# Hashed attention with two MLPs: first pair's bits written straight into the operand, query hashes on four column groups, every second weight tile of the second MLP converted during the second job

## The chip, the cores and the metric

One core of a Trainium2 chip runs the whole program; the other cores are idle. The metric is the device time of one execution in microseconds (us), and the profile is one execution taken by the hardware profiler. Engines: PE is TensorE, DVE is VectorE, ACT is ScalarE, POOL is GpSimd, SP is SyncE, which here only issues DMAs. ACT issues a few DMAs too. Each engine runs its own instructions strictly in the order in which the program was written.

## The reference

```python
q_bits = (einsum('bhsd,dk->bhsk', q, proj) > 0)          # 6 bits a row, k_bits likewise
mask = q_bucket[:, :, :, None] == k_bucket[:, :, None, :]
scores = where(mask, scale * q @ k.T, -1e9)
attn = softmax(scores); x = attn @ v                     # 2 batches, 8 heads, 768 rows, 64 wide
h = x @ w_in;  g = s * relu(h)**2 + b;   y = g @ w_out   # first MLP: 1536 tokens, 512 -> 2048 -> 512
h = y @ w2_in; g = h * clip(h + 3, 0, 6) / 6; out = g @ w2_out
```

Everything is float32. The weights arrive as raw 64-bit words.

## The kernel before, in words

**Split products.** PE takes each float32 operand in two parts, a rounded one ("hi") and a rest ("lo"). ACT makes the hi parts, POOL and DVE the lo parts.

**Attention.** The 1536 rows are four units of 384 query rows (two per batch), and each unit has four pairs of heads: 16 pairs, number g. A pair's operands are four tiles. `KA` holds k_hi in partitions 0 to 63 and from 64 on the hash bits of the keys; `QA` has q_hi and the hash bits of the queries; `KB` and `QB` hold the lo parts and a shifted copy. A matmul over `KA` and `QA` then adds a huge number wherever two hashes differ. So a pair's first score matmul (L466) waits for its key bits, its query bits, `k_shift` (a DMA that copies k_hi into the upper half of `KB`) and `k_lo`, `q_lo` on POOL. Each pair has six slots; a slot is scores with a row maximum on DVE (L472), then the transposed scores (L519), exponentials on ACT (L525, tile `P`), a cast (L532, `pt`), the rest on POOL (L538) and the product with v (L548). `v_scale` is seven DVE instructions that wait for the load of v (`vP`).

**Hash bits.** `bits_mm` (L382) multiplies a projection of 32 columns with 384 columns of k or q at a time; each such matmul uses its own group of 32 output columns of PE (four for k, two for q). `bits` (L391) compares with 0 on DVE into a tile `bits`; for the keys `bits_big` (L397) scales it on ACT. Then DMAs move the rows: `bits_in` (L415, four DMAs for each of the first four pairs), `bits_out` (L407, two DMAs for q; L403 stores key bits in DRAM for the second unit of the batch, which fetches them in L419). The four pairs of the first unit have operand sets of their own, set up by `ones_rows` (L329, L330).

**MLPs.** Tokens of a unit pass through an MLP as one job of 32 weight tiles of 128x512; the eight jobs run in the order of `ORDER`: MLP 1 on units 0 and 1 (jobs 0 and 1), MLP 2 on units 0 and 1 (jobs 2 and 3), and so on. A tile's 12 matmuls (L681) take some 2.1 us. In the first 16 tiles of a job each result goes through ACT, DVE, ACT, DVE (L692 to L716) into `G`. The first job of each MLP (job 0 and job 2) converts its weights from 64-bit words: load `wr` (L612, 512 KB), two ACT operations (`w_exp` L618, `w_low` L627), two DVE operations (L631, L636), and a store of the float32 tile (L642, 256 KB). Later jobs fetch that (L646). A tile sits in one of four buffers `wf` until `w_hi` on ACT (L651) and `w_lo` on POOL (L657) have split it.

**Order.** `Plan` is a list scheduler in the kernel's own Python. Each step has an engine, a due time, a duration and the things it needs, and the plan writes all instructions in the order that it finds; DMAs are put on SP's queue, some on ACT's. Any changed step or duration may reorder every engine.

Of the kernel before, what the change touches and what calls it, by code (L numbers as in the profile page):

```python
# [226 lines left out]
def attn_moe_moe2(ctx, tc, qT, kT, vT, proj, cvec, eye, w1_in, w1_out, w2_in, w2_out, out):  # L227
# [36 lines left out]
    cv = const.tile([128, 4], F32, name="cv")  # L264
# [5 lines left out]
    ones = const.tile([128, 32], F16, name="ones")  # L270
    hbit = {(b, h): dr_p.tile([128, 384], F32, name=f"kb{b}{h}") for b in range(2) for h in range(4)}
# [28 lines left out]
    def bank(g):  # L300
        if small_ring(g) == "mm":
            return ps["mm"].tile([128, 512], F32, tag="mm", name="small")
        return ps["S"].tile([128, 512], F32, tag="S", name="S")
# [54 lines left out]
    def k_lo(g):  # L358
        nc.gpsimd.tensor_tensor(out=operand(g, "KB")[0:64], in0=pd[g]["k"], in1=operand(g, "KA")[0:64].bitcast(F32), op=ALU.subtract)  # L359
# [17 lines left out]
    def bits_mm(g, nm):  # L377
        n = 4 if nm == "k" else 2
        src = pd[g][nm][0:64].rearrange("p h n -> p (h n)")
        bp = bank(g)  # L380
        for i in range(n):
            nc.tensor.matmul(out=bp[32 * i:32 * i + 32, 0:384], lhsT=projb, rhs=src[:, 384 * i:384 * i + 384],  # L382
                             start=True, stop=True)
        pd[g][nm + "ps"] = bp

    def bits(g, nm):


        n, i = (128, 0) if nm == "k" else (64, 1)
        bt = ev_p.tile([128, 384], F32R, tag="r" if nm == "k" else "o", name="bits")  # L390
        nc.vector.tensor_scalar(out=bt[0:n], in0=pd[g][nm + "ps"][0:n, 0:384], scalar1=0.0, scalar2=cv[0:n, i:i + 1],  # L391
# [7 lines left out]
    def bits_out(g, nm):  # L399
        bt = pd[g][nm + "bt"]  # L400
        if nm == "k":
            u, hp = pairs[g]
            queue[0].dma_start(out=hbit[units[u][0], hp], in_=bt.bitcast(F32))  # L403
        else:
            dst = operand(g, "QA").rearrange("p h n -> p (h n)").bitcast(F32)
            for i in range(2):
                queue[0].dma_start(out=dst[64:64 + 2 * NB, 384 * i:384 * i + 384],  # L407
                                  in_=bt[32 * i:32 * i + 2 * NB].bitcast(F32))

    def bits_in(g):  # L410
        u, hp = pairs[g]
        if g < 4:
            dst = operand(g, "KA").rearrange("p h n -> p (h n)").bitcast(F32)
            for i in range(4):
                queue[0].dma_start(out=dst[64:64 + 2 * NB, 384 * i:384 * i + 384], in_=pd[g]["kbt"][32 * i:32 * i + 2 * NB].bitcast(F32))  # L415
            return
# [354 lines left out]
    for e in range(4):  # L771
        add("DVE", 9.0 * e - 14.0, 2.0, ones_rows, (e,), gives=[("ones", e)])
# [3 lines left out]
    for g in range(NP):  # L776
# [7 lines left out]
        add("DMA", t, (0.6, 1.7), load_k, (g,), acq=[(kH, g)], gives=[("k", g)])  # L784
        add("DMA", t, (1.2, 1.7), load_q, (g,), acq=[(qD, g)], gives=[("q", g)])
        add("ACT", t, 1.47, k_hi, (g,), needs=free + [("k", g)], gives=[("kh", g)])
        add("DMA", t, (0.6, 1.7), k_shift, (g,), needs=[("kh", g)], gives=[("kd", g, 0)])
# [192 lines left out]
```

## Time and profile before

| | |
|---|---|
| median of 3 runs | 876.61 us (875.98 to 876.70) |
| profiled execution, its own time | 876.93 us |
| its span (first to last instruction) | 875.1 us |
| PE busy / ACT / POOL / DVE | 95% / 66% / 65% / 53% of the span |
| jobs 0, 1, 2, 3 begin their matmuls at | 101.8, 261, 354, 457 us |

Busy shares are means over the whole span. What a change is worth is read from the stage where it stands: from 0 to 101.8 us there is attention alone, then jobs with attention slots between their tiles, and in the last third nearly only weight tiles.

### The profile page before, as it was taken

How to read it: one execution, taken by the hardware profiler on the slowest of the kernel's cores; microseconds unless marked ns; L12 is line 12 of the kernel's file. 1: busy time of each engine (PE TensorE's matmuls, PEld its weight loads, DVE VectorE, ACT ScalarE, POOL GpSimd, SP SyncE). 2: the span in 40 equal slices, each digit the busy share in tenths (PEclk: the TensorE clock that was granted, in tenths of full speed). 3: DMA queues.
4: the chain of work that ended last, by engine and by line, in shares of the span. 5: the costliest groups of instructions: out<-in, count | busy, mean ns of one | idle time of the engine just before them, and what ended most of it. 6: DMA issues, size and time to landing. Idle time of an engine off the chain costs nothing.

```text
span 875.1 us, 15178 instructions
## 1 busy us (share of the span) xinstructions
PE 828.4 (95%) x5430; PEld 735.1 (84%) x5430; DVE 464.2 (53%) x838; ACT 579.0 (66%) x977; POOL 572.3 (65%) x388
## 2 busy tenths in 40 slices
PE   6779898999999799998999999999999999999998
PEld 2446677869786799887899987999998888999998
DVE  7668758788755741897365404530465422521520
ACT  5359959898785554898887635753687464743752
POOL 5467757678687256455877656566588675666664
PEclk9779999999999899999999999999999999999999
DMA  8874356677668435787855434444334323444442
GB/s 189 164 185 149 110 157 189 219 225 224 199 181 175 125 105 188 266 264 269 273 172 156 129 113 129 135 133 126 119 96 116 79 79 88 129 126 128 124 142 76
DMA packets 74987, 136.72 MB, mean 156 GB/s; under 512 B 20288, under 2 KB 30880, under 8 KB 74912
## 3 DMA queue, kind: packets, MB, share of 16 engines
q1 hardware_dynamic: 73516, 133.09, 52.2%
q10 hardware_dynamic: 1396, 2.66, 1.3%
q8 instruction: 43, 0.70, 0.4%
q14 instruction: 32, 0.26, 0.1%
HBM read 103.86 MB, written 21.54 MB: 143 GB/s over the span
## 4 chain that ended last, share of the span: by engine, by line
PE 80%; DVE 7%; DMA 5%; ACT 4%; issue 2%; POOL 1%; SPq 1%; ACTq 0%; DVEq 0%; POOLq 0%
PE mm L681 58%; PE T L519 6%; PE S L466 6%; PE pv L548 6%; DMA kH<-k_t 2%; PE S L559 1%; DMA wr<-w_in 1%; PE S L382 1%; DMA vP<-v_t 1%; PE pv L580 1%; DVE nh L472 1%; DVE wf L631 1%; ACT wf L627 1%; DVE am L425 1%; DVE KA L330 1%
## 5 line engine op out<-in xcount | busy, mean ns | idle before, releaser
L657 POOL TENSOR_TENSOR wl<-wf,wh 128x512 fp32r<-128x512 f32 x256 | 330.2, 1292 | 197.5 <-ACT wh L651 183.2
L681 PE MATMUL mm<-X,wh 128*128 128x384 f32 x1024 | 267.4, 342 | 13.4 <-DVE G L713 6.8
L681 PE MATMUL mm<-G,wh 128*128 128x384 f32 x1024 | 265.5, 340 | 0.0
L651 ACT CAST wh<-wf 128x512 fp32r<-128x512 f32 x256 | 157.7, 617 | 107.9 <-PE mm L681 77.3
L538 POOL TENSOR_TENSOR pt<-P,pt 128x768 f16<-128x768 f32 x96 | 159.8, 1668 | 79.4 <-ACT pt L532 71.1
L681 PEld LDWEIGHTS mm<-X,wh 128*128 128x128 f32 x1024 | 186.0, 191 | 23.9 <-DVE G L713 9.8
L681 PEld LDWEIGHTS mm<-G,wh 128*128 128x128 f32 x1024 | 182.6, 188 | 11.4 <-issue 10.4
L681 PE MATMUL mm<-X,wl 128*128 128x384 f32 x512 | 173.7, 339 | 0.0
L681 PE MATMUL mm<-G,wl 128*128 128x384 f32 x512 | 171.5, 335 | 0.0
L472 DVE TENSOR_REDUCE nh<-S 128x1 f32<-128x384 f32 x192 | 103.3, 552 | 90.9 <-PE S L466 89.8
L525 ACT ACTIVATE P<-T 128x768 f32<-128x768 f32 x96 | 78.0, 812 | 49.3 <-PE T L519 46.8
L681 PEld LDWEIGHTS mm<-X,wl 128*128 128x128 f32 x512 | 97.4, 190 | 0.0
L681 PEld LDWEIGHTS mm<-G,wl 128*128 128x128 f32 x512 | 96.1, 188 | 0.0
L466 PE MATMUL S<-KA,QA 76*128 76x384 f32 x192 | 72.8, 379 | 14.2 <-DVE nh L472 10.4
L532 ACT CAST pt<-P 128x768 f16<-128x768 f32 x96 | 80.0, 834 | 7.9 <-PE pv L548 5.9
L519 PE MATMUL T<-QA,KA 108*128 108x384 f32 x192 | 69.0, 359 | 3.4 <-ACT pt L532 1.2
L466 PE MATMUL S<-KB,QB 128*128 128x384 f32 x192 | 67.4, 351 | 0.3 <-DMA KB<-KA 0.3
L519 PE MATMUL T<-QB,KB 128*128 128x384 f32 x192 | 65.7, 342 | 0.0
L466 PEld LDWEIGHTS S<-KA,QA 76*128 76x128 f32 x192 | 37.4, 195 | 31.2 <-DVE nh L472 21.1
L548 PE MATMUL pv<-pt,vt 128*64 128x384 f16 x576 | 63.3, 344 | 0.2 <-DVE X L596 0.2
L631 DVE SCALAR_TENSOR_TENSOR wf<-wm,wf 128x512 int32<-128x512 int32 x64 | 43.9, 686 | 33.2 <-ACT wf L627 26.7
L359 POOL TENSOR_TENSOR KB<-kH,KA 64x1536 fp32r<-64x1536 f32 x14 | 48.6, 3473 | 11.4 <-ACT KA L353 11.2
(358 smaller groups left out, 942.0 us busy)
## 6 DMA issues: line engine op xcount, KB each, us to landing
wf<-w SPq DMA_DIRECT2D x192, 256.0 KB
wr<-w_in SPq DMA_DIRECT2D x32, 512.0 KB
w<-wf SPq DMA_DIRECT2D x64, 256.0 KB
wr<-w_out SPq DMA_DIRECT2D x31, 512.0 KB
KB<-KA SPq DMA_DIRECT2D x16, 384.0 KB
qD<-q_t SPq DMA_DIRECT2D x28, 192.0 KB
kH<-k_t SPq DMA_DIRECT2D x13, 384.0 KB
U<-ur SPq DMA_DIRECT2D x16, 192.0 KB
```

What stands on the lines that cost most here:

```text
L359: nc.gpsimd.tensor_tensor(out=operand(g, "KB")[0:64], in0=pd[g]["k"], in1=operand(g, "KA")[0:64].bitcast(F32), op=ALU.subtract)
L466: nc.tensor.matmul(out=sp[:, 0:NQ], lhsT=operand(g, Q)[0:n, h, 128 * t:128 * t + 128], rhs=operand(g, K)[0:n, h, NQ * j:NQ * j + NQ], star ...
L472: nc.vector.reduce_max(out=maxima[g % 2][:, j, c:c + 1], in_=sd.pop((s, j))[:, 0:NQ], axis=AX.X, negate=True)
L519: nc.tensor.matmul(out=tp[:, j, 0:NQ], lhsT=operand(g, K)[0:n, h, c:c + 128], rhs=operand(g, Q)[0:n, h], start=(a == 0), stop=(a == 1))
L525: nc.scalar.activation(out=P, in_=td.pop((g, k))[:, :, 0:NQ], func=AF.Exp, scale=0.125)
L532: (nc.scalar.copy if THI(g) == "ACT" else nc.vector.tensor_copy)(pd[g][h][:, 0, 2 * i:2 * i + 2], pd[g]["P", k])
L538: e.tensor_tensor(out=pt[:, 1, 2 * i:2 * i + 2], in0=pd[g].pop(("P", k)), in1=pt[:, 0, 2 * i:2 * i + 2], op=ALU.subtract)
L548: nc.tensor.matmul(out=d["pv"][64 * h:64 * h + 64, 0:NQ], lhsT=vt[:, vc, 64 * h:64 * h + 64], rhs=d[h][:, a, c], start=(c == 0 and n == 0) ...
L631: nc.vector.scalar_tensor_tensor(out=d["wf"], in0=d["mt"], scalar=-2147483648, in1=d["wf"], op0=ALU.bitwise_and, op1=ALU.bitwise_or)
L651: nc.scalar.copy(hi.rearrange("p a b -> p (a b)"), wq[key]["wf"])
L657: nc.gpsimd.tensor_tensor(out=lo.rearrange("p a b -> p (a b)"), in0=d["wf"], in1=d["hi"].rearrange("p a b -> p (a b)").bitcast(F32), op=AL ...
L681: nc.tensor.matmul(out=a, lhsT=w[:, k, :], rhs=src[k][:, xi, :], start=(k0 + k == 0 and p == 0), stop=(k0 + k == nk - 1 and p == 2))
```

## The change

For pair 0 the key and query bits go from PSUM to their operand rows in six DVE instructions of 12 partitions (no ACT scaling, no bit DMAs); the keys use a negated projection `projk`, and the stored copy for pair 4 is read from `KA`. Query hashes of pairs 4 to 15 use four column groups of 192 columns in place of two of 384, and four DMAs in place of two. `k_lo` is cut into one instruction per head. 12 warm-up matmuls stand in place of 16. Odd tiles of MLP 2 are converted during job 1, stored, and fetched in job 2. Several durations in the planner's table are smaller.

```diff
-WARM = (16, 6)
+WARM = (12, 6)
...
+EARLY = 2
...
-    def k_lo(g):
-        nc.gpsimd.tensor_tensor(out=operand(g, "KB")[0:64], in0=pd[g]["k"], in1=operand(g, "KA")[0:64].bitcast(F32), op=ALU.subtract)
+    def k_lo(g, h):
+        nc.gpsimd.tensor_tensor(out=operand(g, "KB")[0:64, h], in0=pd[g]["k"][:, h], in1=operand(g, "KA")[0:64, h].bitcast(F32), op=ALU.subtract)
...
     def bits_mm(g, nm):
-        n = 4 if nm == "k" else 2
+        n, w = (2, 384) if nm == "q" and g < 4 else (4, 384 if nm == "k" else 192)
...
     def bits(g, nm):
...
+        if g == 0:
+            ps_, dst = pd[g][nm + "ps"], operand(g, "KA" if nm == "k" else "QA").rearrange("p h n -> p (h n)")
+            for i in range(4 if nm == "k" else 2):
+                r = slice(32 * i, 32 * i + 2 * NB)
+                a, b = (cv[r, 4:5], cv[r, 5:6]) if nm == "k" else (0.0, cv[r, 1:2])
+                nc.vector.tensor_scalar(out=dst[64:64 + 2 * NB, 384 * i:384 * i + 384], in0=ps_[r, 0:384], scalar1=a, scalar2=b,
+                                        op0=ALU.is_ge if nm == "k" else ALU.is_gt, op1=ALU.mult if nm == "k" else ALU.subtract)
+            return
...
-            for i in range(2):
-                queue[0].dma_start(out=dst[64:64 + 2 * NB, 384 * i:384 * i + 384],
-                                  in_=bt[32 * i:32 * i + 2 * NB].bitcast(F32))
+            w = 384 if g < 4 else 192
+            for i in range(2 * NQ // w):
+                queue[0].dma_start(out=dst[64:64 + 2 * NB, w * i:w * i + w],
+                                  in_=bt[32 * i:32 * i + 2 * NB, 0:w].bitcast(F32))
...
+        if g == 4:
+            queue[0].dma_start(out=operand(g, "KA")[64:64 + 2 * NB].rearrange("p h n -> p (h n)").bitcast(F32), in_=hrow)
+            return
...
+            pre = (m, jn) == (1, first[1]) and i % EARLY == EARLY - 1
             if jn == first[m]:
...
+                if pre:
+                    ck, tw, use, order = (100, i), M[jn - 1][0] + i * M[jn - 1][1], past(jn - 1, i, 0), []
...
-                last = [("wf", ck, 2)]
...
+                last = [("wf", ck, 1 if pre else 2)]
...
-            else:
...
+            if jn != first[m] or pre:
```

How the order moves is shown at three places. First, SP's queue from the shift of pair 0 on, before. `KB_151<-KA_149` is the shift of pair 0, `KA_153` and `QA_154` are operands of pair 1, `KA_160` and later ones of pairs 2 and 3; `kb` are key bits going to DRAM.

```order
L356 DMA KB_151<-KA_149 64x1536
L415 DMA KA_149<-bits 12x384 x4
L407 DMA QA_150<-bits 12x384 x2
L335 DMA kH<-k_t 64x1536
L403 DMA kb_117<-bits 128x384
L343 DMA qD<-q_t 64x2x384 x2
L356 DMA KB_155<-KA_153 64x1536
L335 DMA kHx<-k_t 64x1536
L356 DMA KB_162<-KA_160 64x1536
L415 DMA KA_153<-bits 12x384 x4
L403 DMA kb_118<-bits 128x384
```

The same stretch of SP's queue after; pair 0 has `KA_151`, `KB_153`, pair 1 has `KA_155`, `QA_156`, `KB_157`.

```order
L362 DMA KB_153<-KA_151 64x1536
L349 DMA qD<-q_t 64x2x384 x2
L362 DMA KB_157<-KA_155 64x1536
L416 DMA kr<-KA_151 12x1536
L341 DMA kH<-k_t 64x1536
L341 DMA kHx<-k_t 64x1536
L433 DMA KA_155<-bits 12x384 x4
L349 DMA qDx<-q_t 64x2x384 x2
L420 DMA kb_120<-bits 128x384
L425 DMA QA_156<-bits 12x384 x2
L355 DMA vP<-v_t 128x768
```

The six bit DMAs of pair 0 are gone from the queue, and one store `kr` has come; pair 1's own six stand in the same order as before, behind fewer others.

Second, ACT at the end of job 1, before: `X<-mm` are the outputs of the job's last tiles, `wh` the casts of its weight tiles, `wm` and `wf` the two conversion steps.

```order
L651 CAST wh<-wf 128x512 x3
L719 CAST X_112<-mm 128x384
L651 CAST wh<-wf 128x512 x4
L719 CAST X_113<-mm 128x384
L651 CAST wh<-wf 128x512 x4
L618 ACTIVATE wm<-wr 128x512
```

The same place after:

```order
L663 DMA w_13_220<-wf 128x512
L740 CAST X_113<-mm 128x384
L667 DMA wf<-w_23_198 128x512
L672 CAST wh<-wf 128x512
L663 DMA w_15_222<-wf 128x512
L639 ACTIVATE wm<-wr 128x512
L648 ACTIVATE wf<-wr 128x512
L672 CAST wh<-wf 128x512
L546 ACTIVATE P<-T 128x768
L639 ACTIVATE wm<-wr 128x512
```

Conversions, exponentials and three DMA issues now stand between the casts, where there were only casts.

Third, ACT early in job 2 (`r__` and `G` are its activation steps), before:

```order
L692 ACTIVATE r__4511<-mm,three 128x384
L651 CAST wh<-wf 128x512
L618 ACTIVATE wm<-wr 128x512
L707 CAST G_1378<-mm 128x384
L627 ACTIVATE wf<-wr 128x512
L692 ACTIVATE r__4547<-mm,three 128x384
L651 CAST wh<-wf 128x512
L525 ACTIVATE P<-T 128x768
L707 CAST G_1379<-mm 128x384
L618 ACTIVATE wm<-wr 128x512
```

And after, in the same tiles:

```order
L713 ACTIVATE r__4851<-mm,three 128x384
L672 CAST wh<-wf 128x512
L728 CAST G_1347<-mm 128x384
L648 ACTIVATE wf<-wr 128x512
L713 ACTIVATE r__4884<-mm,three 128x384
L639 ACTIVATE wm<-wr 128x512
L672 CAST wh<-wf 128x512
L728 CAST G_1348<-mm 128x384
L713 ACTIVATE r__4909<-mm,three 128x384
L672 CAST wh<-wf 128x512
L639 ACTIVATE wm<-wr 128x512
```

Before, nearly every tile carries a conversion and some an exponential; after, fewer conversions stand there and no exponential. Counted over ACT's whole order: between the casts of job 2's first and 17th tile stand 16 `wm` and 4 `P` before, 11 `wm` and 1 `P` after. Between the casts of job 1's first tile and job 2's first tile stand 2 `wm` and 2 `P` before, 15 `wm` and 11 `P` after.

## Rows read from the trace of the kernel before

**Rows 1.** Busy time of each engine by stage: PE, PEld, DVE, ACT, POOL, clock, DMA
```profile
0.00:101.80 101.80, 80.09 (x545) 52.38 (x545) 78.41 (x149) 64.51 (x87) 64.61 (x37) 0.90 0.66 166
101.80:261.00 159.20, 151.46 (x1107) 126.53 (x1106) 116.56 (x212) 132.94 (x217) 116.92 (x73) 0.99 0.64 193
261.00:320.30 59.30, 52.41 (x329) 44.41 (x327) 37.04 (x68) 33.09 (x60) 30.75 (x21) 0.91 0.60 141
...
354.00:406.20 52.20, 45.52 (x240) 42.14 (x239) 46.47 (x84) 48.93 (x91) 28.19 (x22) 0.97 0.80 262
...
457.00:875.10 418.10, 414.73 (x2687) 390.21 (x2685) 150.41 (x267) 242.01 (x426) 273.08 (x196) 1.00 0.41 117
```
**Rows 2.** Timeline of SP's queue, first 30 us: start, us, issues
```profile
9.76 3.25 SPq L415 DMA_DIRECT2D KA<-bits  x4
13.11 1.48 SPq L407 DMA_DIRECT2D QA<-bits  x2
...
21.20 3.54 SPq L415 DMA_DIRECT2D KA<-bits  x4
...
27.20 1.63 SPq L407 DMA_DIRECT2D QA<-bits  x2
28.93 0.46 SPq L349 DMA_DIRECT2D vP<-v_t  x1
```
**Rows 3.** Busy tenths of the DMA engines, 0 to 40 us, one digit a us
```profile
DMA  0069999999998200989999999678519999988951
```
**Rows 4.** Timeline of all engines, first 36 us: start, us, [idle before and releaser]
```profile
5.35 1.50 PE L382 MATMUL small<-kH,projb 64*32 64x384 f32 x8 [5.35 <-DMA projb<-proj_]
...
8.56 0.62 DVE L391 TENSOR_SCALAR bits<-small,cv 128x384 fp32r<-128x384 f32 x1
...
13.20 1.86 PEld L375 LDWEIGHTS <-eyes 128*128 128x128 f16 x9 [0.28 <-issue]
...
15.37 0.41 PE L466 MATMUL S<-KA,QA 76*128 76x384 f32 x1
...
16.24 0.85 PE L382 MATMUL small<-kHx,projb 64*32 64x384 f32 x8
...
29.96 0.41 PE L466 MATMUL S<-KA,QA 76*128 76x384 f32 x1 [3.47 <-DMA QA<-bits]
...
32.71 0.95 DVE L425 TENSOR_REDUCE am<-vP 128x1 f32<-128x768 f32 x1 [1.47 <-DMA vP<-v_t]
...
36.42 0.69 PE L466 MATMUL S<-KA,QA 76*128 76x384 f32 x1 [2.78 <-DVE nh L472]
```
**Rows 5.** Chain that ended last, near 230 us: start, us, what
```profile
231.39 0.77 PE S L382 x4
```
**Rows 6.** Waits of PE from 354 to 457 us
```profile
PE mm L681 <- DVE G L716: 6.4, 7, 2.8
```
**Rows 7.** Waits of PE from 261 to 354 us
```profile
PE mm L681 <- DVE G L713: 5.0, 3, 2.7
```
**Rows 8.** Groups by line, shapes apart: busy, mean ns of one, idle before and releaser
```profile
L657 POOL TENSOR_TENSOR wl<-wf,wh 128x512 fp32r<-128x512 f32 x256 | 330.2, 1292 | 197.5 <-ACT wh L651 183.2 <-DVE mm L700 3.2 <-DVE wf L636 3.0
...
L651 ACT CAST wh<-wf 128x512 fp32r<-128x512 f32 x256 | 157.7, 617 | 107.9 <-PE mm L681 77.3 <-POOL wl L657 27.1 <-DMA wf<-w 1.9
...
L532 ACT CAST pt<-P 128x768 f16<-128x768 f32 x96 | 80.0, 834 | 7.9 <-PE pv L548 5.9 <-DVE wf L631 0.8
L525 ACT ACTIVATE P<-T 128x768 f32<-128x768 f32 x96 | 78.0, 812 | 49.3 <-PE T L519 46.8 <-POOL pt L538 2.2
...
L631 DVE SCALAR_TENSOR_TENSOR wf<-wm,wf 128x512 int32<-128x512 int32 x64 | 43.9, 686 | 33.2 <-ACT wf L627 26.7 <-ACT wm L618 4.2 <-issue 1.3
L627 ACT ACTIVATE wf<-wr 128x512 int32<-128x512 uint16 x64 | 42.8, 668 | 0.1
L618 ACT ACTIVATE wm<-wr 128x512 f32<-128x512 f32 x64 | 40.6, 635 | 7.1 <-DVE wf L636 4.0 <-DMA wr<-w_in 3.0
```
**Rows 9.** What SP's queue waited for, whole span
```profile
SPq L646 <- POOL wl L657: 319.3, 175, 8.6
```

More of the change, by code (lines that the diff above doesn't have):

```diff
@@ L263, in attn_moe_moe2 @@
     projb = const.tile([64, 32], F32, name="projb")
-    cv = const.tile([128, 4], F32, name="cv")
+    projk = const.tile([64, 32], F32, name="projk")
+    cv = const.tile([128, 6], F32, name="cv")
     s_c, b_c = cv[:, 2:3], cv[:, 3:4]
@@ L298, in small_ring, with bits_ring, bank @@
         return "mm" if g < 4 else "S"
-    def bank(g):
-        if small_ring(g) == "mm":
+    def bits_ring(g, nm):
+        return "S" if (g, nm) == (0, "q") else small_ring(g)
+    def bank(g, ring=None):
+        if (ring or small_ring(g)) == "mm":
             return ps["mm"].tile([128, 512], F32, tag="mm", name="small")
@@ L377, in bits_mm @@
     def bits_mm(g, nm):
-        n = 4 if nm == "k" else 2
+        n, w = (2, 384) if nm == "q" and g < 4 else (4, 384 if nm == "k" else 192)
         src = pd[g][nm][0:64].rearrange("p h n -> p (h n)")
-        bp = bank(g)
+        bp = bank(g, bits_ring(g, nm))
         for i in range(n):
-            nc.tensor.matmul(out=bp[32 * i:32 * i + 32, 0:384], lhsT=projb, rhs=src[:, 384 * i:384 * i + 384],
+            nc.tensor.matmul(out=bp[32 * i:32 * i + 32, 0:w], lhsT=projk if nm == "k" and g == 0 else projb, rhs=src[:, w * i:w * i + w],
                              start=True, stop=True)
@@ L399, in bits_out @@
     def bits_out(g, nm):
+        u, hp = pairs[g]
+        if g == 0:
+            queue[0].dma_start(out=hrow, in_=operand(g, "KA")[64:64 + 2 * NB].rearrange("p h n -> p (h n)").bitcast(F32))
+            return
         bt = pd[g][nm + "bt"]
         if nm == "k":
-            u, hp = pairs[g]
             queue[0].dma_start(out=hbit[units[u][0], hp], in_=bt.bitcast(F32))
@@ L771, in attn_moe_moe2 @@
     for e in range(4):
-        add("DVE", 9.0 * e - 14.0, 2.0, ones_rows, (e,), gives=[("ones", e)])
+        add("DVE", 9.0 * e - 14.0, 2.0, ones_rows, (e,), needs=[("bits", 0, "q")] if e > 1 else [], gives=[("ones", e)])
     lastT = [("ex", g, k) for g in range(4) for k in range(SPP) if tring(g, k) == "Tx" and SPP * g + k < SPU]
@@ L783, in attn_moe_moe2 @@
         kH, qD = raw_ring(g, "kH"), raw_ring(g, "qD")
-        add("DMA", t, (0.6, 1.7), load_k, (g,), acq=[(kH, g)], gives=[("k", g)])
-        add("DMA", t, (1.2, 1.7), load_q, (g,), acq=[(qD, g)], gives=[("q", g)])
+        add("DMA", t, (0.6, 1.35), load_k, (g,), acq=[(kH, g)], gives=[("k", g)])
+        add("DMA", t, (1.2, 1.35), load_q, (g,), acq=[(qD, g)], gives=[("q", g)])
         add("ACT", t, 1.47, k_hi, (g,), needs=free + [("k", g)], gives=[("kh", g)])
-        add("DMA", t, (0.6, 1.7), k_shift, (g,), needs=[("kh", g)], gives=[("kd", g, 0)])
-        add("POOL", t, 3.5, k_lo, (g,), needs=[("kh", g)], gives=[("kd", g, 1)], rel=[(kH, g, 2 if own else 1)])
+        add("DMA", t, (0.6, 1.35), k_shift, (g,), needs=[("kh", g)], gives=[("kd", g, 0)])
+        for h in range(2):
+            add("POOL", t + 2 * h, 1.78, k_lo, (g, h), needs=[("kh", g)] + ([("qd", 0, 1)] if h and g == 0 else []), gives=[("kd", g, 1 + h)], rel=[(kH, g, 3 if own else 2)])
         add("ACT", t, 0.83, q_hi, (g,), needs=free + [("q", g)], gives=[("qh", g)])
@@ L918, in attn_moe_moe2 @@
         nc.scalar.dma_start(out=cv, in_=cvec)
+        nc.gpsimd.tensor_scalar(out=projk[:, 0:NB], in0=projb[:, 0:NB], scalar1=-1.0, scalar2=None, op0=ALU.mult)
+        nc.gpsimd.tensor_copy(projk[:, NB:32], projb[:, NB:32])
         nc.scalar.dma_start(out=eyes, in_=eye)
```

48 lines of the change are left out of this document (30 added, 18 removed).

## The prediction

> **What bounds the kernel now.** I read the busy time by stage first. The reader is to see how much of each stage PE is not busy (length less PE's busy time) and at which clock it ran. From 457 us on PE is busy for 414.7 of 418.1 us: there only PE's own work can be cut. In job 0 (101.8 to 261) it is idle for 7.7 us. The idle time that something else could give back stands at three places: 21.7 us before 101.8, 6.9 us in the first half of job 1, and 6.7 us in the first half of job 2. The first of these also ran at a granted clock of 0.90 on average, job 1's first half at 0.91 [rows 1]. Then I read the head in order of time. SP spends 3.25 and 1.48 us on issuing pair 0's bit DMAs, and 3.54 and 1.63 us on pair 1's, in one queue with all loads [rows 2]. PE starts pair 0 at 15.37 us, and pair 1 only at 29.96 us, after 3.47 us of idleness that the query bits of pair 1 ended. At 32.71 us DVE had waited 1.47 us for v, with `v_scale` ahead of everything else in its order, and PE's next scores came at 36.42 us after 2.78 us idle, waiting for DVE's maxima [rows 4]. Last I read who is waited for in jobs 1 and 2. In job 2 PE waits 6.4 us for the last step of `G` (L716) [rows 6], and ACT is busy for 48.9 of the 52.2 us in its first half, while it has 26.2 us free in job 1's first half [rows 1]. So ACT, with a conversion in nearly every tile, is what holds up job 2's first half.
>
> **Head.** Pair 0's first scores need four things. The key bits: today the product (1.50 us at the slow clock), 0.62 us on DVE [rows 4], the scaling, and DMAs issued from 9.76 to 14.6 us [rows 2]. After, the loads of k and q change places, so k lands when q does today, which I put at 7.4 us; then come 1.5 us of product and four DVE instructions. A 12-partition compare is not in the trace; its nearest row is the one of 128 partitions, 0.62 us. I take that for each, since a cost in proportion to the partitions (four in 0.24 us) would only help: 7.4 + 1.5 + 2.5 = 11.4 us. The second is the shift of k: its DMA is issued later, near 9 us, but sits behind the same loads, and these keep the DMA engines busy until about 13 us, after which they fall idle until 16 us [rows 3]. So the shift lands near 13.3 us in either order. The third, `k_lo`, has its first head done by then. The fourth is PE itself: 12 warm-up matmuls and the product for pair 1's keys (0.85 us [rows 4]) stand ahead of the scores, and end near 14.3 us. First scores: 14.3 in place of 15.4 us, 1.1 us earlier.
>
> More is won at pair 1. Its query bits stand in SP's queue behind the rest, and pair 0's 4.73 us of issuing [rows 2] are replaced by one store of about 0.5 us. What then comes last is ACT: `bits_big` of pair 1 stands behind the casts of pair 2's queries, near 18.2 us by my count of the loads and casts ahead. From there the queue goes as today: 3.54 us for the key bits, 2.46 us for the two issues between (24.74 to 27.20), 1.63 us for the query bits [rows 2], and 1.13 us from the end of these (28.83) to the scores at 29.96 [rows 4]. 18.2 + 8.8 = 27.0 us: pair 1 starts 3.0 us earlier, the 1.1 us of pair 0 contained. Next `v_scale`: SP issues v right behind, and in DVE's new order four maxima of pair 1 and all bits stand ahead of it, so that part of the 1.47 us wait for v goes; I count 0.7 us. Head: 3.7 us. Bounds: 0, if the time up to 101.8 us takes it back, since the waits there may be for the next loads of v; and 7.3 us, if the wait of 2.78 us at 36.42 and all of the 1.47 us go as well.
>
> **Warm-up.** The same product took 1.50 us at 5.35 us and 0.85 us at 16.24 us, and from 13.20 us the warm-up's weight loads come every 0.21 us (nine in 1.86 us) [rows 4]: there PE had risen from the lower (1.2 GHz) to the higher of its two levels (2.4 GHz). After, PE works from 5.35 us as before and with a shorter gap between its products, so I take the same moment and no cost. The Trainium skill, in "TensorE: Matmul & The Clock Gate", section "Part 1: The HAM clock gate", says that time spent busy releases the clock and not a number of matmuls, and that the moment differs from run to run. By that rule a shorter warm-up may end before the clock rises, where the row with 16 has it rise inside; the sum would then be some 3 us worse, and no run shown here has that case. It is priced from rows as a rival below.
>
> **Query hashes.** Eight records took 1.50 us at the lower level and 0.85 us at the higher [rows 4]. The difference, 0.65 us, is the array's time at the higher level, and 0.85 - 0.65 = 0.20 us does not depend on it. Two column groups for q take 0.77 us on the chain [rows 5], hardly less than four groups for k with 0.85 us: groups run side by side. Half the columns in twice the groups should then save half of 0.65, 0.33 us; at most half of 0.77, 0.39 us; at least nothing, if 192 columns do not run side by side, against which k's four groups speak. Twelve pairs: 4.0 us. Four of them lie after 424 us and count in full; the eight before lie in stages where PE is 5% to 21% idle, and I count four fifths: 1.3 + 2.1 = 3.4 us. Bounds 0 and 4.7. The two more DMAs a pair cost SP about 1.9 us (3.54 for four less 1.63 for two), 23 us in all, behind the 319.3 us that it waits with fetches for `w_lo` [rows 9]; without that cover each would delay a fetch by 1.9 us.
>
> **Jobs 1 and 2.** A conversion takes ACT 0.635 + 0.668 = 1.30 us, a slot's exponential and cast 0.812 + 0.834 = 1.65 us [rows 8]. In job 2's first half the new order has five conversions and three slots fewer: 6.5 + 4.9 = 11.4 us less of ACT's 48.9, so 37.5 us, well under PE's 45.5 us [rows 1], which itself falls by the moved slots. Of 6.7 us idle I let 5.2 go, and 0.3 us of clock. Job 1 takes them up. Its first half has ACT idle for 26.2 us and is given six conversions and three slots (12.7 us). But these stand between the steps of `G`, for which PE waits 5.0 us there already [rows 7], and SP has 16 more loads and 16 more stores to order. I charge 2 us for both halves: 3.5 us net. Bounds: up to 9 us, if job 1's waits shrink too as slots are spread over it; below nothing, by the ring (first rival). The rest costs nothing: `k_lo` in halves and the two instructions for `projk`, because POOL has 37 us free before 101.8 us; DVE's 2.4 us more for pair 0, because it sets up pairs 2 and 3 later instead; 16 more fetches (256 KB each), because job 2, at a DMA share of 0.80 [rows 1], loses 16 loads of 512 KB. Were job 1's queue full, a fetch would be late by its landing, which is the ring's case.
>
> **Sum.** 876.9 (the profiled execution) - 3.7 - 3.4 - 3.5 = 866.3 us. That execution lies 0.3 us above the median of the runs, so I predict 866.0 us. Runs of this kernel spread by 0.7 us, so 0.2% (1.8 us) is about what can be told from no change.
>
> **Rivals.**
> *Slower: the ring of four `wf` buffers in job 1.* A fetched tile holds a buffer for its landing plus 0.62 + 1.29 us; a converted one from `w_low` over two DVE steps until its store has landed, 0.67 + 2 x 0.69 + 0.6 between them = 2.7 us plus a landing [rows 8]. The nearest landing is that of v in the head, 28.93 to 32.71 us, 3.8 us [rows 2, 4]. Two fetched and one converted tile need 3 x 3.8 + 2 x 1.9 + 2.7 = 17.9, over four buffers 4.5 us for two tiles, against 4.2 us of PE's work; attention moved into job 1 adds about 1.5 us to the latter. So it is hidden until a landing takes some 5.5 us. At 7 us it would be 6.9 us against 5.7, 1.2 us for each of 16 pairs of tiles, 19 us: 866.0 + 19 = 885 us. For it: fetches already wait for `w_lo` 175 times [rows 9], and stores now stand on ACT's queue in job 1, ahead of casts. Against it: job 2 did 32 loads and stores at a DMA share of 0.80 [rows 1], and the wait that stands out there is for `G` [rows 6].
> *Head given back.* The next loads of v, or DVE, end the waits up to 101.8 us as before: 866.0 + 3.7 = 869.7 us. That DVE held PE up at 36.42 us [rows 4] speaks for it; that SP's queue is shorter speaks against.
> *Late clock.* If the warm-up ends cold, pair 0's scores and the bits beside them run at half speed; eight records would again take 1.50 for 0.85 us [rows 4], and with some four times that work there, about 3 us: 869.0 us.
> *Job 2 unchanged.* Its waits go to job 1 in full, and only head and hashes remain: 866.0 + 3.5 = 869.5 us; with the head lost too, 873.2 us.
> *All upper bounds.* 876.6 - 7.3 - 4.7 - 9 = 855.6 us.
>
> **Numbers.** The forecast's own case (862 to 868.5 us) 0.40, head lost 0.14, late clock 0.07, job 2 unchanged 0.10, better than forecast (855 to 862) 0.10, head and job 2 lost 0.06, ring or another new wait in the order 0.13. Half of the last but one, and 0.03 of the last, would come to lie within 0.2%: faster 0.84, same 0.06, slower 0.10. The range leaves out the slow cases and the last of the good ones: 856 to 874 us.
>
> **What the new profile would show.** Right: first scores near 14.3 us and pair 1's near 27 us with little idle time before them; q products of about 0.45 us on the chain; PE's wait for L716 in job 2's first half under 2 us and ACT below 80% there; PE idle in job 1 at most 2 us more. Wrong: long waits of PE for `wh` or `wl` in job 1, SP waiting there for stores, DVE waiting for v again before 50 us, or the first matmul of job 0 still near 101 us.

## The result, and the profile after

The changed kernel takes 885.46 us (median of 881.37, 888.34, 884.51 and 886.42), beside 876.3 us for the kernel before in the same session: a ratio of 1.0103, 95% interval 1.0058 to 1.0148. It is slower by some 9 us; the forecast was 866.0 us. The profiled execution was the fastest of the four, 881.37 us with a span of 879.3 us, so what it shows is the milder case. In all that follows, medians and ranges leave out one slow execution each of e6, e9 and e11.

The busy time by stage, after (columns as in [rows 1]; the stages begin at the first matmuls of job 0 at 98.1 us, job 1 at 251.3, job 2 at 355.1 and job 3 at 449.5):
```profile
0.00:98.10 98.10, 78.34 (x540) 50.17 (x541) 77.86 (x147) 64.75 (x84) 69.75 (x46) 0.95 0.72 159
98.10:251.30 153.20, 145.73 (x1100) 122.21 (x1099) 113.41 (x204) 124.81 (x211) 107.67 (x72) 0.99 0.64 198
251.30:310.10 58.80, 52.58 (x296) 46.99 (x295) 42.00 (x84) 44.21 (x78) 34.38 (x25) 0.94 0.78 226
310.10:355.10 45.00, 44.50 (x305) 42.45 (x304) 25.58 (x43) 32.08 (x53) 28.20 (x21) 1.00 0.83 252
355.10:412.90 57.80, 44.36 (x276) 40.31 (x275) 39.11 (x70) 42.97 (x79) 30.50 (x23) 0.94 0.73 236
...
449.50:879.30 429.80, 425.96 (x2760) 397.01 (x2758) 156.85 (x281) 247.19 (x432) 273.45 (x201) 1.00 0.39 112
```
Set against [rows 1], the head is 3.7 us shorter, and job 1's first half starts 9.7 us earlier (251.3 for 261.0). Job 1 now keeps the DMA engines busy for 0.78 of its first half in place of 0.60, and for 0.83 of its second half. Then job 2's first half takes 57.8 us in place of 52.2, with PE idle for 13.4 us in place of 6.7, although ACT is now only 74% busy there (42.97 of 57.8). The lead of 9.7 us is gone where job 2 begins (355.1 for 354 us), partly because attention moved too: counted by its transposed scores (`T`), job 1 has 12 slots beside it in place of none, and job 2 has 6 in place of 12.

What PE waits for in that stretch (355.1 to 412.9 us): the wait for `G` that was to fall below 2 us [rows 6] grew.
```profile
PE mm L702 <- DVE G L737: 7.8, 6, 3.3
PE S L487 <- ACT ds L585: 3.2, 1, 3.2
PE mm L702 <- POOL wl L678: 1.5, 2, 0.8
```
And the chain of work that ended last, 340 to 381 us: a store, a fetch that waited for a store, a store, a fetch, with up to 11.82 us for 256 KB.
```profile
348.95 4.49 DMA w<-wf
...
353.51 5.71 DMA wf<-w
...
361.10 7.75 DMA w<-wf
...
368.92 11.82 DMA wf<-w
```
The two longest of PE's waits stand right behind these landings. ACT reaches `w_low`, which needs a free `wf` buffer, and stands for 4.76 us until a store has landed; then its cast waits 2.32 us for the fetch above. PE waits for ACT's `ds` and for `G`, which come behind them in ACT's order.
```profile
377.10 0.66 ACT L648 ACTIVATE wf<-wr 128x512 int32<-128x512 uint16 x1 [4.76 <-DMA w<-wf]
378.50 0.45 PE L487 MATMUL S<-KA,QA 76*128 76x384 f32 x1 [3.22 <-ACT ds L585]
380.76 0.62 ACT L672 CAST wh<-wf 128x512 fp32r<-128x512 f32 x1 [2.32 <-DMA wf<-w]
382.40 1.01 PE L702 MATMUL mm<-X,wh 128*128 128x384 f32 x2 [3.28 <-DVE G L737]
```
So 6.5 of the 13.4 us go back to landings that ACT waited for, not to ACT's work.

To compare stages between kernels whose work stands in different places, I count **lost time**: the time up to a point, less what PE's matmuls up to there take at the higher clock with nothing to wait for (by their spacing in the traces: 0.173 us for a matmul of the MLPs, 0.178 for one of the scores, 0.77 or 0.46 for a query product, and so on). This work is 775.1 us before and 770.5 after: 3.7 less for twelve products, 0.9 less for four warm-ups. Lost time by stage, worked out from one profile each and good to half a microsecond, in us. The changed kernel, e2 and e13 have one order, and the first two differ by some 4 us in the head and in job 1, 3 in job 2, so smaller differences in one column say little:
```
                              head  job 0  job 1  job 2  jobs 3-7   sum
before                        39.1   19.7   14.0   13.4    10.1    96.3
after                         37.3   19.9   13.7   19.0    14.9   104.8
after + gap (e2)              41.5   19.4   17.3   16.2    13.1   107.5
 "  one load (e13)            38.9   19.9   12.8   15.3    13.2   100.1
 "  no early (e4)             40.9   21.2    6.2   14.7    13.5    96.5
 "  no early, 8 wf (e10)      44.6   17.1    1.4   10.9    11.2    85.2
 "  8 wf (e6)                 44.0   18.6   10.7    7.1    12.4    92.8
old head, early, 8 wf (e12)   40.1   20.0   12.5    5.0    11.1    88.7
old head, 8 wf (e16)          52.5   17.7    4.3   12.9    12.0    99.4
```
"Old head" has pair 0's bits by copies, `k_lo` whole and 16 warm-ups as before; "no early" is EARLY at 33; "8 wf" is eight `wf` buffers. Jobs 3 to 7 lose 4.8 us more than before as well, 1.8 of which e2 wins back; most of the rest lies in job 3, where PE shows no wait, and its cause stays open.

### The profile page after: what moved, and what is told of

Its sections match the earlier page's. It is cut to its first block, busy times and chain, and to the rows that moved or that the text cites. A ratio compares the mean times of both kernels' runs of the same rounds, so it can differ in the third digit from the quotient of the medians.

```text
span 879.3 us, 15350 instructions
## 1 busy us (share of the span) xinstructions
PE 828.1 (94%) x5474; PEld 735.7 (84%) x5474; DVE 464.6 (53%) x842; ACT 581.5 (66%) x976; POOL 574.3 (65%) x406
## 4 chain that ended last, share of the span: by engine, by line
PE 74%; DMA 10%; DVE 7%; ACT 4%; issue 2%; SPq 2%; POOL 1%; ACTq 0%; DVEq 0%; POOLq 0%
PE mm L702 53%; PE T L540 6%; PE S L487 6%; PE pv L569 5%; DMA wf<-w 3%; DMA vP<-v_t 2%; DMA wr<-w_in 2%; DMA w<-wf 1%; PE S L580 1%; PE pv L601 1%; DVE wf L652 1%; DVE nh L493 1%; DMA kb<-bits 1%; DVE wf L657 1%; ACT P L546 1%
## 5 line engine op out<-in xcount | busy, mean ns | idle before, releaser
L702 PE MATMUL mm<-G,wh 128*128 128x384 f32 x1024 | 269.5, 344 | 0.0
L569 PE MATMUL pv<-pt,vt 128*64 128x384 f16 x576 | 61.5, 333 | 0.0
L365 POOL TENSOR_TENSOR KB<-kH,KA 64x768 fp32r<-64x768 f32 x28 | 51.0, 1829 | 5.8 <-ACT KA L359 5.3
```

Source lines behind the costliest of these rows:

```text
L365: nc.gpsimd.tensor_tensor(out=operand(g, "KB")[0:64, h], in0=pd[g]["k"][:, h], in1=operand(g, "KA")[0:64, h].bitcast(F32), op=ALU.subtract)
L569: nc.tensor.matmul(out=d["pv"][64 * h:64 * h + 64, 0:NQ], lhsT=vt[:, vc, 64 * h:64 * h + 64], rhs=d[h][:, a, c], start=(c == 0 and n == 0) ...
L702: nc.tensor.matmul(out=a, lhsT=w[:, k, :], rhs=src[k][:, xi, :], start=(k0 + k == 0 and p == 0), stop=(k0 + k == nk - 1 and p == 2))
```

## The experiments

Each was timed in turn with the kernel before, whose median was 872.8 to 874.9 us in these sessions. Between sessions I compare ratios; 0.001 is 0.9 us. "Same order" means that every engine has the same instructions in the same order as the kernel it is compared with; where the planner counts the edit, it finds a new order for everything.

**Where the operands lie (e1, e2).** `projk` moves everything behind it in SBUF by 128 bytes, but not `G`, which lies at the other end. Both edits only move addresses.
```diff
     projb = const.tile([64, 32], F32, name="projb")
+    gap = const.tile([64, 32], F32, name="gap")
     cv = const.tile([128, 4], F32, name="cv")
```
(e1, on the kernel before)
```diff
     projk = const.tile([64, 32], F32, name="projk")
+    gap = const.tile([128, 96], F32, name="gap")
     cv = const.tile([128, 6], F32, name="cv")
```
(e2, on the changed kernel)


> The kernel before with one unused tile of 128 bytes per partition ahead of cv, so that X, wf, wh, wl and the operands stand 128 bytes higher, as in the changed kernel, while G stays; no instruction moves. Theory A (where the operands lie sets the rate of the second-layer matmuls): the spacing of second-layer matmuls in the jobs without attention goes from 173.3 to about 176 ns, first-layer tiles stay at 173.3, and the time rises by about 4 us to 880 (ratio 1.0045, between 1.003 and 1.006). Rival (the spacing came from the granted clock of that execution, or from the new order of instructions): 876.3, ratio 1.000 within 0.0015, spacing 173.3 in both layers.

> The changed kernel with one unused tile of 384 bytes per partition behind projk, so that X, wh and wl stand 512 bytes higher than in the kernel before; no instruction moves. Theory A (placement): second-layer spacing back to 173.3 ns and about 4 us less than the changed kernel's 885.5, so 881.5 (ratio to before 1.006). Rival: 885.5 (ratio 1.0103) and second-layer spacing still near 176.

Measured: e1 877.20 us, ratio 1.0014 (0.9991 to 1.0038); e2 884.32, ratio 1.0111 (1.0079 to 1.0142). PE's groups in a second half of job 6, for the kernel before (771.8 to 805 us), then for e1 (773.3 to 807 us):
```profile
L681 PE MATMUL mm<-G,wh 128*128 128x384 f32 x128 | 32.5, 334 | 0.0
```
```profile
L682 PE MATMUL mm<-G,wh 128*128 128x384 f32 x127 | 32.7, 338 | 0.0
```
Their starts lie 173.3 ns apart before and 176.0 in e1 (means over 191 spacings each); after e2's gap it is 173.3 again, and first-layer tiles stay within 0.1 ns of 173.3 throughout. Job 6 takes 67.1 us in e1 and 66.6 in e2 and before, from its first matmul to job 7's. So theory A holds for the rate, but a job has 192 such matmuls: 0.5 us a job and at most 4 us in eight, of which 1.5 us can be seen in the three jobs without attention. In the whole kernel it is lost in the spread (e1 against before: 1.2 us by the ratio, where some 4 were expected; e2 against after: none; e4 against e3: 1.2 us).

**Without early conversions (e3, e4).**
```diff
-EARLY = 2
+EARLY = 33
```


> The changed kernel with EARLY at 33, so that no tile of the second MLP is converted beside job 1 and job 2 converts all 32, as before. Theory B (the 16 early conversions, with four wf buffers that wait for stores and landings, cost job 2 what the head and job 1 had won, 7 to 9 us): 876 to 878.5 without anything else changed (ratio 0.9995 to 1.0025), the waits of PE for G or weights at 360 to 400 us fall to under 2 us. Rival (the early conversions are worth their 3.5 us and the loss lies elsewhere, in the head or in the clock): 887 to 889 (ratio 1.012 to 1.015).

> The changed kernel with both edits: no early conversions and the 384 byte gap. If A and B both hold and add, 872 to 874.5 (ratio 0.995 to 0.998), which would be faster than the kernel before. If only A holds: about 881 to 885. If only B holds: 876 to 878.5. If neither: 885 or more.

Measured: e3 874.41 us, ratio 1.0003 (0.9987 to 1.0019); e4 873.24, ratio 0.9983 (0.9969 to 0.9997). By the ratios, taking the early conversions out brings back 9 us (e3 against after) or 11 (e4 against e2). That is what theory B asked for or a little more, but not where it said: job 1 loses 6.2 us in place of 17.3 (e4, e2), job 2 hardly changes, and PE's wait for `G` at 360 to 400 us, which was to fall below 2 us, is 6.4 us in e3, what job 2 of the kernel before had [rows 6].

**More `wf` buffers (e5, e6).** In e5 the pool has eight and the planner counts four.
```diff
-    wf_p = ctx.enter_context(tc.tile_pool(name="wf", bufs=WF_BUFS))
+    wf_p = ctx.enter_context(tc.tile_pool(name="wf", bufs=8))            # e5
-... WF_BUFS ... = 2, 3, 4, 3, 3, 7
+... WF_BUFS ... = 2, 3, 8, 3, 3, 7                                      # e6
```


> The changed kernel with the 384 byte gap (884.3 us in its own run) and eight wf buffers in place of four, while the planner still counts four, so that every engine runs the same instructions in the same order and only the waits for a free wf buffer can go. Theory C (the early conversions lose because wf buffers come free late, behind stores and landings): the ACT wait of w_low for a store falls from 7.5 us to under 1, PE's waits for G and weights around job 2's start shrink, and the time falls by 5 to 10 us to 874.5 to 879. Rival 1 (the order itself loses: conversions before attention on ACT and DVE, more data on the DMA queues, the chain store, landing, fetch): the same time within 1.5 us, 883 to 886.

> The changed kernel with the 384 byte gap and eight wf buffers, which the planner counts too and orders anew. Theory C (ring): 873 or less, since the order can use the room as well. Rival 1 (order and load of the early conversions): 880 to 886, whatever the ring. A fall to between 873 and 880 would say that ring and order share the loss.

Measured: e5 880.25 us, ratio 1.0068 (1.0044 to 1.0092); e6 875.27, ratio 1.0008 (0.9977 to 1.0039), between 869.4 and 881.9 from run to run. In e2 ACT waits for stores between 251 and 420 us, in e5 it doesn't any more:
```profile
ACT wf L649 <- DMA w<-wf: 7.5, 6, 3.7
```
So these are the waits for a free buffer, and they are worth about 4 us of the 11 (the intervals of e2 and e5 overlap a little; ACT's waits for fetches grow by 3 us): theory C is a part of it, no more.

**One edit alone (e7, e8, e9).** e7 gives the kernel before the four-group query hashes, in the same order; e9 takes them from e2, in the same order; e8 takes them from e4 and plans anew.
```diff
-        n = 4 if nm == "k" else 2
+        n, w = (2, 384) if nm == "q" and g < 4 else (4, 384 if nm == "k" else 192)
...
-            for i in range(2):
+            for i in range(2 * NQ // w):
```


> The kernel before with the query hashes of pairs 4 to 15 on four column groups (the bodies of three steps alone, with two more copies per pair on the queue), every engine in the order of before. The term of the forecast: 12 products that take 0.46 in place of 0.77 us, less 3.5 us, ratio 0.996 (0.995 to 0.9975). Rival (the freed PE time lies in waits for other engines or the two more copies per pair cost it back): ratio 1.000 within 0.0015.

> The changed kernel without early conversions, with the gap, and with the query hashes on two column groups again: what is left is the head (first pair's bits, warm-up of 12, the split of k_lo, the new transfer times in the planner). The head's term of the forecast, 3.7 us: 870.8 (ratio 0.996). Theory D (the head gives nothing, what it wins at the first exponential it loses in waits at 20 to 30 us and in the cold clock): 874.5 to 877, ratio 1.000 to 1.003, and job 0's first matmul at 101 to 103 us as before.

> The changed kernel with the 384 byte gap, its query hashes of pairs 4 to 15 back on two column groups, every engine in the order of the changed kernel: the counterpart, in the other order, of the run that gave the kernel before these hashes alone. Theory E (the hashes are worth the 3.5 us that they free on PE, and what the run on the order of before lost came from a colder clock): 887 to 889 against 884.3 with them. Rival (the freed time lies in waits, and two more copies for each pair cost as much): 882 to 885.

Measured: e7 877.88 us, ratio 1.0042 (1.002 to 1.0064): slower, against both theories. e8 877.18, ratio 1.0036 (1.0009 to 1.0063), 4.6 us more than with the hashes; what it has left of the change is the head and the planner's durations, and job 0's first matmul comes at 107.3 us, so theory D is near (874.5 to 877), and the head's 3.7 us are not there. e9 887.21, ratio 1.0137 (1.0089 to 1.0184), 2 to 3 us more than with them, with intervals that overlap. In e7's profile PE's work is some 3.5 us less and its lost time some 3 us more, and job 0 begins at 103.2 us in place of 101.8, after a head where no instruction changed before 65 us. The granted clock over its first 98 us was 0.86 beside 0.90 before, and the median over whole runs 0.976 beside 0.980. So theory E fits, but that the clock is the cause of e7's loss is argued, not shown.

**The remaining corners (e10, e11, e12).** e10 is e4 with eight counted buffers; e11 is e6 with 16 warm-ups, same order; e12 is the old head with the hashes, the early conversions, the planner's transfer times and eight counted buffers.
```diff
-        for _ in range(n):
+        for _ in range(16 if n == 12 else n):            # e11
```


> The changed kernel without early conversions, with the gap, with eight wf buffers that the planner counts: the fourth of the four (early or not, four or eight buffers: 884.3, 873.2, 876.5 are known). Theory C (the four buffers hurt because of the early conversions): within 2 us of 873.2, so that eight buffers are worth 8 us with early conversions and under 2 without. Rival (four buffers are short in any order): 866 to 869, as much gained as with early conversions.

> The kernel with early conversions and eight wf buffers (876.5 us median, 869.4 to 882.8 from run to run), with 16 warm-up matmuls in the place of 12, every engine in the same order. Theory F (the warm-up that got shorter leaves the clock low in the head, and the spread is that clock): the mean granted clock rises from 0.973 to 0.978 or more and the median falls to 870 to 873. Rival (the head's clock hangs on later waits, not on four matmuls of the warm-up): 876 to 878, the spread unchanged.

> The head of the kernel before (first pair's bits by copies, warm-up of 16, no projk and so no gap), with the hashes, the early conversions and the planner's transfer times of the changed kernel, and eight wf buffers that the planner counts. Theory D (the head edits give nothing or cost): no slower than the same with the new head (876.5), 870 to 876. The forecast's head term (3.7 us gained by the new head): 880. If head, hashes and early conversions were all worth what the forecast said, this would be 869.5.

Measured: e10 860.97 us, ratio 0.9846 (0.981 to 0.9882), which beats both kernels and both ranges named for it; e11 875.71, ratio 1.0018 (0.999 to 1.0045), between 870.7 and 878.9; e12 865.65, ratio 0.9897 (0.9859 to 0.9934), below every value named for it. Theory C falls as the main cause: without early conversions eight buffers seem worth more (12 us) than with them (9). Theory F falls too: four more warm-ups don't lower the median. One case of e6's spread can be followed: in e11's profile job 1 ends 6 us later for its start than in e6's, in the same order (lost time 16.8 us beside 10.7). The chain there runs over a fetch of 12.35 us, but this fetch had landed by 345.9 us, before ACT was free to cast it; ACT stood in front of `vhl`, waiting for the transposed v. The row of e6, then two of e11:
```profile
342.00 0.94 ACT L462 ACTIVATE vhl<-vP,sc 128x768 f16<-128x768 f32 x1 [2.27 <-DMA vt<-vhl]
```
```profile
347.21 0.93 ACT L462 ACTIVATE vhl<-vP,sc 128x768 f16<-128x768 f32 x1 [5.18 <-DMA vt<-vhl]
...
349.81 0.62 PE L703 MATMUL mm<-G,wh 128*128 128x384 f32 x2 [2.94 <-ACT wh L673]
```
PE's 2.94 us are half of the 6. The other half is the clock: in the second half of job 1, e6 had 1.00 granted, and PE was busy for 40.2 us, e11 0.93 and 43.0.
```profile
313.70:355.40 41.70, 40.21 (x233) 38.29 (x228) 27.91 (x52) 26.11 (x45) 20.28 (x16) 1.00 1.04 285
```
```profile
316.40:363.80 47.40, 43.01 (x230) 41.36 (x231) 28.12 (x52) 25.97 (x44) 19.99 (x16) 0.93 0.94 251
```

**Bytes or engine work (e13, e14, e15), and the last corner (e16).** e13: all early tiles use one raw tile. e14, e15: loads alone and engine work alone, put behind `w_hi` of every second tile of job 1.
```diff
+        if key[0] == 100:                                          # e13, in w_load
+            if i == EARLY - 1: queue[0].dma_start(out=rawx, in_=wsrc[m][i]...)
+            wq[key] = {"raw": rawx}
+            return
...
+            nc.sync.dma_start(out=more, in_=wsrc[1][key[1]]...)    # e14
...
+            nc.scalar.activation(out=a..., in_=idle, ...)          # e15: ScalarE
+            nc.scalar.activation(out=b..., in_=idle, ...)
+            nc.vector.scalar_tensor_tensor(out=c, in0=a, ..., in1=b, ...)
+            nc.vector.scalar_tensor_tensor(out=c, in0=a, ..., in1=c, ...)
```


> The changed kernel with the 384 byte gap (884.3), in which the 16 early tiles are all converted from one raw tile that is loaded once: 15 loads of 512 KB are left out beside job 1 and with them the true weights of these tiles; every conversion, store and fetch stays, each engine in the same order. Theory G (the bytes on the DMA queues beside job 1 make fetches and loads land late): 875 to 880, and job 1 shorter by 5 us or more. Rival (ScalarE and VectorE work, or their order): 883 to 886.

> The changed kernel without early conversions, with the gap (873.2), and with 16 further loads of 512 KB beside job 1 whose data nothing reads, one at each second weight tile, on SyncE's queue; the other instructions in the same order. Theory G (bytes beside job 1): 879 to 884. Rival (not the bytes but the engines' work): 872 to 875.

> The changed kernel without early conversions, with the gap (873.2), and with the engine work of 16 conversions beside job 1 without their bytes: two ScalarE and two VectorE instructions on 512 columns at each second weight tile, whose output nothing else reads; the other instructions in the same order. Theory G (bytes): 872.5 to 875. Rival (engine work): 879 to 884.

> The head of the kernel before, the hashes on four column groups, the planner's transfer times of the changed kernel, eight wf buffers that the planner counts, and no early conversions (with them it took 865.7). If early conversions lose under the old head as under the new one (15 us there): 851 to 858. If their loss with the new head came from that order alone: 865 to 870. Against 861.0 with the new head it also tells the head's price: equal if the head is worth nothing.

Measured: e13 875.64 us, ratio 1.0005 (0.9981 to 1.0028); e14 876.20, ratio 1.001 (0.9987 to 1.0033); e15 907.34, ratio 1.0354 (1.0322 to 1.0386); e16 877.50, ratio 1.0024 (0.9997 to 1.0051). Job 1 as a whole, columns as in [rows 1], for e2, e13, e4 and e14:
```profile
255.40:362.70 107.30, 96.34 (x598) 88.95 (x596) 67.55 (x127) 76.25 (x130) 62.55 (x45) 0.97 0.79 230
```
```profile
252.90:355.80 102.90, 96.45 (x598) 89.15 (x598) 67.44 (x127) 76.05 (x130) 62.40 (x45) 0.97 0.63 175
```
```profile
255.40:344.10 88.70, 86.38 (x550) 80.96 (x549) 47.38 (x93) 54.60 (x97) 56.05 (x42) 0.98 0.63 176
```
```profile
256.10:346.70 90.60, 86.34 (x550) 80.50 (x549) 47.23 (x94) 54.95 (x97) 55.20 (x41) 0.98 0.88 258
```
With 15 loads gone, every engine in the order of e2, the DMA engines fall from 0.79 to 0.63 busy and the ratio by 0.0106, some 9 us, clear of both intervals. By the two profiles job 1 is 4.4 us and job 2 0.9 us shorter; another 2.8 us lie in the head, which the edit doesn't touch, and job 1 of the changed kernel itself, 103.8 us in the order of e2, is only 0.9 us longer than e13's. So that the loads cost is shown, 5 to 9 us, and where it is lost only roughly. The edit takes away the conversions' own waits for their loads as well as the bytes (in e2 some 2 us of ACT's time). Loads added alone (e14 beside e4) cost 2 to 3 us, with intervals that overlap a little and under what theory G asked, although job 1's DMA share rose to 0.88, above that of e2: the share alone doesn't set the price. e15 shows the opposite of theory G, and more than its rival: PE's waits in job 1 and just behind it (255 to 380 us) have one group that stands out,
```profile
PE mm L710 <- DVE G L742: 13.6, 6, 4.8
```
and the clock there is 0.89. But this work was put in without being planned, and its two engines wait for each other at every tile; it says that ScalarE and VectorE are not free beside job 1's steps of `G`, not what planned conversions cost there. e16, finally, is 11 us slower than the same with early conversions (e12), outside both ranges named for it: under the old head they gain.

**Order or buffers (e17, e18).** e17 is e4 with eight buffers, same order; e18 is the kernel before with eight that the planner counts.

> The changed kernel without early conversions, with the gap (873.2), and with eight wf buffers while the planner counts four: every engine in the same order. If the 12 us that eight counted buffers gave are waits for a free buffer that go: 861 to 866. Theory H (they are the other order that the planner found): 872 to 874.5.

> The kernel before with eight wf buffers that the planner counts, so in a new order, and nothing else. If four buffers are short in any order: 862 to 868. Theory H (each new order is worth some us up or down by itself, the buffers little): anything from 868 to 882, and a head that is several us off the 101.8 us of before at job 0's first matmul.

Measured: e17 873.17 us, ratio 0.9985 (0.9971 to 0.9999); e18 875.69, ratio 1.0019 (1.0003 to 1.0036), with job 0's first matmul at 118.4 us. With the order kept, the buffers are worth nothing without early conversions, so e10's 12 us come only with its new order; whether that order would keep them with four buffers was not run. Theory H holds in both (e18 begins job 0 at 118.4 us). The planner's new durations stand in every run but e1, e7 and e18, `k_lo` by head in every run of the new head; neither was run alone.

## Why the prediction was wrong

The step that failed is "Jobs 1 and 2": 3.5 us were to be won, and the kernel with the early conversions is 9 to 11 us slower than the kernel without (after against e3, e2 against e4). Of the 19.5 us between forecast and result, 12 to 15 stand in this step. Some 6 or 7 more stand in the head and the hashes, which together bring nothing (e3) to 1.5 us (e4) of their 7.1 where the early conversions are out. What the step on jobs 1 and 2 left out:

- **Bytes.** It set the 16 further fetches against 16 loads that leave job 2, and never priced job 1's own queue, which was given the 16 loads of 512 KB and as many stores. The DMA share of job 1's first half rose from 0.60 to 0.78; stores and fetches on the chain took 4.5 to 11.8 us, and the 15 loads account for 5 to 9 us (e13). The prediction wrote of a full queue that a fetch would be late by its landing, and set nothing for it in the sum.
- **The ring.** The slower rival named the place, and its 885 us was what came out, but its mechanism carries only 4 us: that much goes when the same order has eight buffers (e5). That the number was met is luck. Bytes and ring overlap, since a store that lands sooner also frees its buffer sooner.
- **The order.** Nor is the sum of it a property of the conversions. Ratios of the six corners with four-group hashes:
```
                       early    no early
new head, 4 buffers   1.0111     0.9983
new head, 8 buffers   1.0008     0.9846
old head, 8 buffers   0.9897     1.0024
```
Early conversions cost 11 us, cost 14 us, or gain 11, and the new head costs 10 us or gains 16. A price for an edit that changes sign with its neighbours is the price of the order that the planner found around it. The forecast summed three edits as if everything else kept its place; the planner moves everything. Attention, for one, has 12 slots beside job 1 in the changed kernel, none before, 6 in e4, e10 and e12. From order to order, lost time goes from 1.4 to 17.3 us in job 1 and from 5.0 to 19.0 in job 2, more than any of the three terms. Which feature of e10's order makes job 1 run with PE busy for all of its 81.6 us stays open.

The other steps:

**Head.** The 3.7 us were there in the profiled execution (98.1 us in place of 101.8), but not by the path described. k landed later than was taken: its product began at 8.96 us, not 7.4. First scores came at 15.88 us, not 14.3, and pair 1's at 32.66, not 27:
```profile
8.96 1.50 PE L388 MATMUL small<-kH,projk 64*32 64x384 f32 x8 [3.02 <-DMA kH<-k_t]
10.39 4.78 PE L381 MATMUL pv<-eyes 128*128 128x512 f16 x12
10.52 2.75 DVE L400 TENSOR_SCALAR KA<-small,cv 12x384 fp32r<-12x384 f32 x4 [3.31 <-PE small L388]
14.31 0.95 DVE L446 TENSOR_REDUCE am<-vP 128x1 f32<-128x768 f32 x1 [1.04 <-DMA vP<-v_t]
...
15.10 0.85 PE L388 MATMUL small<-kHx,projb 64*32 64x384 f32 x8
...
15.88 0.45 PE L487 MATMUL S<-KA,QA 76*128 76x384 f32 x1
...
20.14 0.84 PE L388 MATMUL small<-qDx,projb 64*32 64x384 f32 x4 [3.29 <-DVE bits L405]
...
22.71 0.88 PE L487 MATMUL S<-KA,QA 76*128 76x384 f32 x1
...
32.66 0.41 PE L487 MATMUL S<-KA,QA 76*128 76x384 f32 x1 [0.34 <-issue]
```
Pair 0's `v_scale` stood in the way, not pair 1's: VectorE waited for v at 14.31 us with pair 1's bits queued behind it, and PE waited 3.29 us for these; a wait for v came back at 54.17 us, 3.84 us long. The four compares took 0.69 us each, near the 0.62 assumed. And the gain doesn't repeat: five profiles of this head's order (after, e2, e5, e9, e13) have job 0's first matmul at 98.1, 102.5, 98.7, 103.7 and 99.7 us, mean 100.6; three of the old one (before, e1, e7) at 101.8, 102.3 and 103.2, mean 102.4. That is 2 us, half of the term, inside a spread of more than 5. The clock has a part in it that the prediction didn't price: the first 98 us before, after and in e2, the latter two in the same order, had 0.90, 0.95 and 0.83 granted.
```profile
0.00:98.00 98.00, 76.29 (x505) 49.93 (x506) 75.27 (x145) 61.94 (x84) 63.08 (x37) 0.90 0.67 168
```
```profile
0.00:98.00 98.00, 78.24 (x540) 50.07 (x541) 77.86 (x147) 64.65 (x84) 69.75 (x46) 0.95 0.72 159
```
```profile
0.00:98.00 98.00, 82.76 (x497) 52.33 (x498) 72.68 (x142) 61.41 (x79) 65.99 (x44) 0.83 0.65 156
```
The spread of 0.7 us that the prediction took from three runs was far too small too: the kernel before ran between 871 and 883 us in these sessions.

**Warm-up.** The warm-ups' weight loads came every 0.43 us, the pace of the lower level, up to 14.21 us; then the pace quickened, and the product behind them took 0.85 us, at the higher level.
```profile
13.78 0.15 PEld L381 LDWEIGHTS <-eyes 128*128 128x128 f16 x1 [0.27 <-issue]
14.21 0.15 PEld L381 LDWEIGHTS <-eyes 128*128 128x128 f16 x1 [0.28 <-issue]
14.57 0.10 PEld L381 LDWEIGHTS <-eyes 128*128 128x128 f16 x1 [0.21 <-issue]
```
So the clock rose in the tenth of 12 warm-ups, near 14.5 us; before it was near 13.2 us, in the seventh of 16. It was not the same moment. That agrees with the rule cited from the Trainium skill, "TensorE: Matmul & The Clock Gate", section "Part 1: The HAM clock gate": time releases the clock, not a number of matmuls. The late-clock rival was near the scene (12 end just behind the clock's rise), and pair 0's first scores ran at the higher level; behind PE's wait of 3.29 us the clock was low again (0.88 us for scores at 22.71, 0.45 at 15.88). Four more warm-ups bring nothing (e11).

**Query hashes.** The product fell to 0.46 us as said, on the chain of the changed kernel:
```profile
529.12 0.46 PE S L388 x8
```
The time freed on PE is real; in the whole kernel it came out as 4.6 us less (e8, planned anew), 2 to 3 less (e9) and 3.7 more (e7), so the size is not settled.

**The signs named in advance.** ACT below 80% in job 2's first half came true (74%) without the wait for L716 (now L737) going: ACT's load was not what held it up, the landings that it waited for were. PE's idle time in job 1 stayed at some 7 us, as hoped. Two signs of being wrong came true as well: VectorE's wait for v before 50 us (at 14.31 us), and SP waiting for stores, 13.8 us in seven waits between 251 and 413 us.
```profile
SPq L667 <- DMA w<-wf: 13.8, 7, 5.0
```

## What to carry to other kernels

Where a planner sets the order, an edit has two effects, its own price and a new order; measure the first with the order kept (same planner costs, other bodies or buffers), and expect the second to be worth more than a term of a few us: here ratios from 0.9846 to 1.0111 around edits that were priced at 0.4% each. Work that is moved beside another stage takes its bytes along. Before its engines' time, price the landings that an in-order engine of the receiving stage will stand waiting for; the DMA share there is a warning, not the price (in e14 loads raised it from 0.63 to 0.88, and job 1 grew by 1.9 us).

## What the hardware showed

Matmuls whose moving operand is `G` start 176.0 ns apart when `wh` and `wl` lie at 96 modulo 512 bytes and `G` at 480, and 173.3 ns when all lie at 480; first-layer tiles, whose `X` moves with the weights, keep 173.3. It is the same to 0.1 ns in jobs 4, 6 and 7 of e1 and in those of before and e2, and a constant of 128 bytes far away is enough to bring it about. Why, no run here shows.

A fetch of 256 KB took 12.35 us from issue to landing at 333.6 us of e11 and 4.61 us at 362.5, with the DMA engines 0.94 busy on average between 316 and 364 us.
```profile
333.58 12.35 DMA wf<-w
...
362.52 4.61 DMA wf<-w
```
The runs of e6, the same order with four warm-ups fewer, spread by some 12 us.

One head, in one order, began job 0 between 98.1 and 103.7 us in five executions, with 0.83 to 0.95 of the clock granted over its first 98 us.
